# Chunked attention and a top-1 mixture of experts on one core: an early proposal for the first expert, and the turn from attention to experts in a hand-written order

## The chip, the core and the metric

One core of a Trainium2 chip runs the whole program. The metric is the device time in microseconds of one execution; lower is better. Work is spread over TensorE (PE, its weight loads shown apart as PEld), VectorE (DVE), ScalarE (ACT), GpSimd (POOL) and SyncE (SP, which here only issues DMAs).

## The reference, cut to what matters

```python
# attention: B=4, H=8, S=768, D=64, chunks of 32 queries
for c in range(nc):
    k_ctx = k[:, :, l_start:r_end]            # 16 keys to the left, 8 to the right
    k_full = np.concatenate([mem_k, k_ctx], axis=2)   # and 8 memory keys
    scores = scale * np.matmul(q_c, k_full.transpose(0, 1, 3, 2))
    a = softmax(scores)
    out[:, :, c_start:c_end] = np.matmul(a, v_full)
# mixture of experts: N=3072 tokens, D=512, E=8 experts, F=1024
logits = x @ w_gate + modality_bias[modality_id]
e_idx = np.argmax(logits, axis=1)
for e in range(E):
    mask = e_idx == e
    h = np.maximum(x[mask] @ w1[e], 0.0)
    out[mask] = gate_w[mask, None] * (h @ w2[e])
```

Only the expert of the highest logit is computed for a token, so tokens have to be grouped by expert on the chip. Counted on the reference's own inputs, three experts get tokens: expert 7 has 735 of the first two batches, 1100 of the first three and 1505 in all; expert 5 has 578, 933 and 1288; expert 2 has 223, 271 and 279.

## The kernel before, in words

**Attention.** A unit is two heads of one batch (16 units, 4 for each batch), and each unit has two half steps; the main loop (`for i in range(n + 2)`) runs over the 32 half steps and two more. In half step i TensorE does the scores of i, transposes the exponents of i-1 (`exps_t`), transposes keys (even half steps, `trans_k`) or queries (odd, `trans_q`) of the next unit, transposes the result of i-2 (`trans_x`) and multiplies the exponents of i-1 with the values (`attend`). ScalarE copies the keys out of PSUM into the block-diagonal tile `kbd` (`store_k`, four copies), the queries (`store_q`) and the results (`xT`), and computes the exponents. VectorE subtracts the maxima (`less_max`) and divides by the sums (`normalize`). GpSimd copies the overlapping rows of the values (`share_v`) and writes the results to DRAM (`xd`). The transposes share four PSUM banks (`bank`); a new one waits until the oldest user has been read.

**Routing.** When a batch's four units are done, `route(b)` is appended to a list, and `pump` takes steps from it between the pieces of attention: a VectorE step counts one, and steps that begin with TensorE work ("pe", "late") wait for the call at the end of a half step. `route` computes logits (L541, L551, L553), the one-hot of the maximum, the rank of each token within its expert (L581 to L586), then one-hot matrices `l1` and `a1` for six tiles of 128 tokens (L654, L656 on VectorE or GpSimd, L646 to L650 on ScalarE), whose product (L664) fills a table of token numbers (L665). The third batch (b = 2) also names the expert with most tokens so far; its number goes to `regs0`, from which SyncE takes the address of the first expert's weights and GpSimd the column of the table.

**Turn.** After half step 29 the rest of the third batch's routing is forced (`pump(99, True)`), `load_w(0, 0)` loads w1 of the first expert (eight pieces `raw`), and `gather(0)` fetches 256 tokens (`xg`). `conv` splits a weight piece into a high part (ScalarE, L726) and a low part (L728, VectorE, or GpSimd in four pieces). `trans` transposes the tokens, `mm1(f)` is one of eight pieces of the first layer (12 matmuls, then ReLU by ScalarE at L804 and the low part by VectorE at L807), `mm2(f)` one of the second layer (6 matmuls, L813). The routing of the fourth batch runs between these, and its table is what `gather(1)` of the next slot reads. `plan_early` and `plan_rest` choose the experts of later slots on VectorE.

**Order.** TensorE, SyncE and GpSimd run in program order everywhere. ScalarE and VectorE run in program order up to half step 26 (`MAN`) and again from `slot(1)`; between the two the framework's scheduler orders them. From slot 1 on everything is slots of `mm1` and `mm2`; a slot's weights stay in place when the next slot has the same expert (a condition on the load).

Of the kernel before, what the change touches and what calls it, by code (L numbers as in the profile page):

```python
# [40 lines left out]
NP3 = 0  # L41
NACT = 2
CPOOL = (10, 12, 13, 14, 15)
MAN = 26
KB = 3
# [8 lines left out]
def tile_chunk_attention_top1_moe(  # L54
# [51 lines left out]
    man = ExitStack()  # L106
    man.enter_context(tc.manual_schedule(engines={mybir.EngineType.Activation, mybir.EngineType.DVE}))
# [81 lines left out]
    regs0 = const.tile([1, 2], I32, name="regs0")  # L189
# [222 lines left out]
    routing, now = [], [0]  # L412

    def pump(k, pe=False):
        k *= KB if routing and routing[0][2] == B - 2 else 1
        while k > 0 and routing:
            g, wait, b, since = routing[0]
            if wait:
                if not pe or now[0] < since + (wait == "late" or b < B - 2) + (wait == "late" and b < B - 2):
                    return  # L420
                pe = False
            r = next(g, None)
            if r is None:
                routing.pop(0)
                return
            routing[0] = (g, r if r != "v" else "", b, now[0])
            k -= r == "v"
# [108 lines left out]
    def route(b):  # L536
# [51 lines left out]
        sx = sm.tile([P, NT, 1], F32, name="sx")  # L588
        nc.vector.reduce_sum(sx, ex, axis=AX.X)
        yield "v"  # L590
        nc.vector.tensor_scalar(sx, sx, 1e-9, None, op0=ALU.add)
        yield "v"
        gt = sm.tile([P, NT, XW - DM], F32, name="gt")
        nc.vector.reciprocal(gt, sx.to_broadcast([P, NT, XW - DM]))
        yield "v"
        with nc.allow_non_contiguous_dma(reason="one gate per token"):
            nc.gpsimd.dma_start(xd[b * S:(b + 1) * S, DM:XW].rearrange("(t p) c -> p t c", p=P), gt)
# [19 lines left out]
        if b == B - 2:  # L617

            cm = sm.tile([P, 1], F32, name="cm")
            cb = sm.tile([P, E], F32, name="cb")  # L620
            nc.vector.tensor_copy(cb, rk[:, NT, :])
            yield "v"
            nc.vector.reduce_max(cm, cb, axis=AX.X)
# [6 lines left out]
            yield "v"  # L630
            nc.vector.tensor_scalar(regs0[:, 0:1], cm[0:1], -1.0, float(E), op0=ALU.mult, op1=ALU.add)
            yield "v"
            nc.vector.tensor_scalar(regs0[:, 1:2], cm[0:1], -float(HI), float(E * HI), op0=ALU.mult, op1=ALU.add)
            yield "v"
# [5 lines left out]
        for t in range(NT):  # L640
# [3 lines left out]
            if b == B - 1 and NP3 <= t < NP3 + NACT:  # L644
# [6 lines left out]
                hot.append((l1, a1))  # L651
                continue
            eng = nc.gpsimd if t < (NPOOL, NPOOL, NPOOL, NP3)[b] else nc.vector
# [4 lines left out]
            hot.append((l1, a1))  # L658
        if b == B - 1:
            plan_early()  # L660
# [37 lines left out]
    def load_w(row, half):  # L698
        if half == 0:
            if row == 0:  # L700
                ev[0] = nc.values_load(regs0[0:1, 0:1], engines=[mybir.EngineType.SP], min_val=0, max_val=E - 1,
                                       skip_runtime_bounds_check_because="the place of one of 8 experts")
            else:
# [6 lines left out]
        kw = {} if row == 0 or row == ROW_X and half == 0 else {"cond": ev[row, "c"]}  # L710
# [84 lines left out]
    def mm1(f, rest=False, whole=True):  # L795
# [11 lines left out]
        nc.vector.scalar_tensor_tensor(hl[:, f], ph, 0.0, hh[:, f].bitcast(F32), op0=ALU.max, op1=ALU.subtract)  # L807
# [90 lines left out]
    for i in range(n + 2):  # L898
        live = i < n
        u, hf = units[i] if live else (NU, i % 2)  # L900
        now[0] = i
        if i == MAN:
            man.close()
# [40 lines left out]
        if i > n:  # L944
            mm1(1)
        if i > n:
            trans_x(*units[i - 2])
        if 1 <= i < n:
            normalize(*units[i - 1])
            pump(1)  # L950
        if i >= 2:
            u2, hf2 = units[i - 2]
            if hf2 == 1 and u2 % 4 == 3:
                routing.append((route(u2 // 4), True, u2 // 4, 0))
        if i == 1:
            routing.append((more_constants(), False, -1, 0))
# [5 lines left out]
        if live and hf == 0:  # L962
            if 0 < u < NU - 3:
                load_qk(u + 3)
            if u >= 1 and u - 1 + NVW < NU:
                load_v(u - 1 + NVW)
        if (u, hf) == (NU - 2, 1):
            while routing:
                pump(99, True)
# [7 lines left out]
            load_w(0, 0)  # L977
            gather(0)
        elif u == NU - 1:
            conv(2 * hf)  # L980
# [117 lines left out]
    ctx.enter_context(tc.manual_schedule(engines={mybir.EngineType.Activation, mybir.EngineType.DVE}))  # L1098
# [53 lines left out]
```

## Time and profile before

| | us |
|---|---|
| median of 3 runs (lowest to highest) | 441.83 (441.26 to 442.32) |
| the profiled execution, its own time | 439.56 |
| its span, first to last instruction | 437.8 |
| busy: PE / DVE / ACT / POOL | 413.5 / 308.4 / 269.1 / 205.5 |

The span is a single stretch of work: attention up to about 130 us, the turn up to about 169 us, then slots. A group of rows has a start in microseconds from the span's start, a duration, the engine, the line, and in brackets the idle time before it and what ended it.

### The profile page before, as it was taken

How to read it: one execution, taken by the hardware profiler on the slowest of the kernel's cores; microseconds unless marked ns; L12 is line 12 of the kernel's file. 1: busy time of each engine (PE TensorE's matmuls, PEld its weight loads, DVE VectorE, ACT ScalarE, POOL GpSimd, SP SyncE). 2: the span in 40 equal slices, each digit the busy share in tenths (PEclk: the TensorE clock that was granted, in tenths of full speed). 3: DMA queues.
4: the chain of work that ended last, by engine and by line, in shares of the span. 5: the costliest groups of instructions: out<-in, count | busy, mean ns of one | idle time of the engine just before them, and what ended most of it. 6: DMA issues, size and time to landing. Idle time of an engine off the chain costs nothing. (4 is left out here: it accounts for less than half of the span.)

```text
span 437.8 us, 11877 instructions
## 1 busy us (share of the span) xinstructions
PE 413.5 (94%) x4053; PEld 354.6 (81%) x4053; DVE 308.4 (70%) x752; ACT 269.1 (61%) x537; POOL 205.5 (47%) x409
## 2 busy tenths in 40 slices
PE   7889999999978989999999999999999999999993
PEld 4667787777756968989798998989898989898982
DVE  7788697796798799848366356767777685959530
ACT  6857878787738555747366456656656656657521
POOL 8998889798588932450154306314031115220101
PEclk9999999999999998999999999999999999999998
DMA  7779988888487110496196968414696304340101
GB/s 203 215 204 259 273 217 251 218 222 215 115 237 248 62 40 17 127 272 188 35 270 214 209 196 271 140 49 147 132 256 203 130 5 158 90 145 1 49 1 48
DMA packets 78308, 69.31 MB, mean 158 GB/s; under 512 B 36764, under 2 KB 64564, under 8 KB 78229
## 3 DMA queue, kind: packets, MB, share of 16 engines
q1 hardware_dynamic: 71488, 48.84, 40.7%
q0 software_dynamic: 5888, 19.41, 14.6%
q8 instruction: 37, 0.61, 0.6%
q14 instruction: 43, 0.34, 0.3%
q10 hardware_dynamic: 852, 0.11, 0.2%
HBM read 81.25 MB, written 16.58 MB: 223 GB/s over the span
## 5 line engine op out<-in xcount | busy, mean ns | idle before, releaser
L803 PEld LDWEIGHTS tr<-xt,w 128*128 128x128 f32 x1152 | 140.9, 189 | 4.6 <-issue 1.9
L803 PE MATMUL tr<-xt,w 128*128 128x256 f32 (+1 forms) x1152 | 142.6, 284 | 1.8 <-ACT xt L761 0.7
L813 PE MATMUL av<-wh,h 128*128 128x512 f32 x384 | 125.7, 399 | 0.0
L813 PEld LDWEIGHTS av<-wh,h 128*128 128x128 f32 x384 | 72.7, 189 | 16.8 <-issue 0.4
L807 DVE SCALAR_TENSOR_TENSOR h<-tr,h 128x256 fp32r<-128x256 f32 x96 | 40.6, 424 | 63.7 <-ACT h L804 45.5
L813 PE MATMUL av<-wl,h 128*128 128x512 f32 x192 | 76.0, 396 | 0.0
L728 DVE TENSOR_TENSOR wl<-raw,wh 128x512 fp32r<-128x512 f32 x91 | 63.3, 695 | 8.5 <-ACT wh L726 1.3
L804 ACT ACTIVATE h<-tr 128x256 fp32r<-128x256 f32 x96 | 36.9, 385 | 52.3 <-PE tr L803 46.0
L838 POOL DMA_INDIRECT out_dram<-o,ix x24 | 24.9, 1037 | 92.6 <-ACT o L834 90.2
L728 DVE TENSOR_TENSOR w<-raw,w 128x512 fp32r<-128x512 f32 x93 | 60.6, 691 | 5.1 <-DMA raw<-in_moe_w_dram 2.5
L301 POOL COPY vw<-vw 24x384 f32<-24x384 f32 (+1 forms) x128 | 60.1, 507 | 8.5 <-DMA vw<-in_v_dram 7.0
L726 ACT CAST wh<-raw 128x512 fp32r<-128x512 f32 x96 | 58.7, 615 | 0.1
L726 ACT CAST w<-raw 128x512 fp32r<-128x512 f32 x96 | 52.9, 622 | 0.0
L343 ACT COPY kbd<-tr 64x672 f32<-64x672 f32 x62 | 48.2, 778 | 4.4 <-PE tr L337 3.3
L813 PEld LDWEIGHTS av<-wl,h 128*128 128x128 f32 x192 | 36.4, 190 | 7.7
L834 ACT ACTIVATE o<-av,gate 128x512 f32<-128x512 f32 x24 | 16.3, 689 | 39.5 <-PE av L813 31.2
L746 POOL DMA_INDIRECT xg<-xd,gx x24 | 27.3, 1137 | 18.3 <-POOL gx L744 5.7
L371 ACT ACTIVATE PT<-tr 128x384 f32<-128x384 f32 x32 | 15.8, 494 | 25.9 <-PE tr L369 25.8
L381 PE MATMUL av<-vw,PT 128*32 128x130 f32 x768 | 28.4, 278 | 1.5 <-ACT PT L371 1.5
L351 PE MATMUL sc<-kbd,qT 128*32 128x128 f32 x768 | 27.4, 275 | 2.3 <-DVE kbd L343 1.3
L381 PEld LDWEIGHTS av<-vw,PT 128*32 128x32 f32 x768 | 19.7, 109 | 6.9 <-issue 4.0
L351 PEld LDWEIGHTS sc<-kbd,qT 128*32 128x32 f32 x768 | 20.6, 109 | 5.6 <-POOL kbd L325 3.0
(250 smaller groups left out, 515.6 us busy)
## 6 DMA issues: line engine op xcount, KB each, us to landing
raw<-in_moe_w_dram SPq DMA_DIRECT2D x192, 256.0 KB
k<-in_k_dram SPq DMA_DIRECT2D x16, 384.0 KB
q<-in_q_dram SPq DMA_DIRECT2D x16, 384.0 KB
xd<-xb POOLq DMA_DIRECT2D x16, 384.0 KB, 4.7
vw<-in_v_dram SPq DMA_DIRECT2D x32, 184.0 KB
xs<-xg SPq DMA_DIRECT2D x14, 256.0 KB
xq<-xs SPq DMA_DIRECT2D x28, 128.0 KB
vw<-in_mem_v_dram SPq DMA_DIRECT2D x32, 48.0 KB
```

The lines of the kernel that those rows point to most:

```text
L301: nc.gpsimd.tensor_copy(vw[r0:r0 + 24, c + 1:c + 1 + w, d], vw[r0 + 32:r0 + 56, c:c + w, d])
L343: copy(dst.rearrange("p c (i j) -> p c i j", j=2)[:, :, :, j], win)
L351: nc.tensor.matmul(sc[32 * j:32 * j + 32, t * P:(t + 1) * P], qT[:, 32 * c:32 * c + 32], kbd[:, c].rearrange("p h m -> p (h m)"), start=Tr ...
L381: nc.tensor.matmul(avb[32 * j:32 * j + 32, t * W:(t + 1) * W], PT[:, t * P + 32 * j:t * P + 32 * j + 32], vw[:, c, 0:W], start=True, stop= ...
L726: nc.scalar.copy(wh[i], raw[i])
L728: (eng or nc.vector).tensor_sub(wl[i][:, s], raw[i][:, s], wh[i][:, s].bitcast(F32))
L746: nc.gpsimd.indirect_dma_start(out=xg[t], out_offset=None, in_=xd[0:rows], in_offset=bass.IndirectOffsetOnAxis(ap=gx[:, t:t + 1], axis=0))
L803: nc.tensor.matmul(pw, wt[i][:, j * P:(j + 1) * P], x[:, c, 0:w], start=(n == 0), stop=(n == 11))
L804: nc.scalar.activation(hh[:, f], ph, AF.Relu)
L807: nc.vector.scalar_tensor_tensor(hl[:, f], ph, 0.0, hh[:, f].bitcast(F32), op0=ALU.max, op1=ALU.subtract)
L813: nc.tensor.matmul(pos[t], x, w[8 + f], start=(f == 0 and n == 0), stop=(f == 7 and n == 2))
L838: nc.gpsimd.indirect_dma_start(out=out, out_offset=bass.IndirectOffsetOnAxis(ap=to[:, t:t + 1], axis=0), in_=outs[t], in_offset=None, boun ...
```

## The change

The first slot's expert is proposed after the second batch (`rege`, `cme`, `ohe`), and its w1 is loaded in half step 26 instead of 29. The third batch keeps the proposal if that expert has at least 256 tokens by then; after half step 29 the load is issued again under the condition that the third batch chose another one. ScalarE and VectorE are in program order throughout. `pump` has a second point in each half step ("mid", before `attend`) at which TensorE work of the third batch's routing may run; `KB` is 2 instead of 3, and the second batch gets half as many steps again. The gate's sum moves behind the one-hot matrices, with a reciprocal of 6 elements and a copy by GpSimd in place of a reciprocal of 96. In the third batch, two of six one-hot tiles go to ScalarE, one (not two) to GpSimd. In the turn, `trans(0)` and `trans(1)` stand before the last `attend`; the order of `conv`, `mm1`, routing and `mm2` is written out: w2 pieces 14 and 15 are split by GpSimd (before 10, 12, 13, 14, 15), piece 7 of w1 too; the table of the fourth batch is filled after `mm2(0)` instead of after `mm2(2)`; the low parts of `mm1(5)` to `mm1(7)` come later (`lows`).

```diff
-CPOOL = (10, 12, 13, 14, 15)
-MAN = 26
-KB = 3
+KB = 2
...
-    man = ExitStack()
-    man.enter_context(tc.manual_schedule(engines={mybir.EngineType.Activation, mybir.EngineType.DVE}))
+    ctx.enter_context(tc.manual_schedule(engines={mybir.EngineType.Activation, mybir.EngineType.DVE}))
...
     def pump(k, pe=False):
-        k *= KB if routing and routing[0][2] == B - 2 else 1
+        k = k * KB if routing and routing[0][2] == B - 2 else k * 3 // 2 if routing and routing[0][2] == B - 3 else k
         while k > 0 and routing:
-            g, wait, b, since = routing[0]
+            g, wait, b, since, point = routing[0]
             if wait:
-                if not pe or now[0] < since + (wait == "late" or b < B - 2) + (wait == "late" and b < B - 2):
+                if b == B - 2 and wait is not True and now[0] < 2 * NU and now <= [since, point]:
+                    return
+                if not pe or pe == "mid" and b != B - 2 or now[0] < since + (wait == "late" or b < B - 2) + (wait == "late" and b < B - 3) or (b, wait) == (B - 2, "late") and now[0] < 2 * NU - 3:
                     return
...
-            if b == B - 1 and NP3 <= t < NP3 + NACT:
+            if b == B - 1 and t < NACT or b == B - 2 and t >= NT - NACT:
...
-            eng = nc.gpsimd if t < (NPOOL, NPOOL, NPOOL, NP3)[b] else nc.vector
+            eng = nc.gpsimd if t < (NPOOL, NPOOL, 1, 0)[b] else nc.vector
...
+        nc.vector.reciprocal(sx, sx)
+        yield "v"
+        gt = sm.tile([P, NT, XW - DM], F32, name="gt")
+        nc.gpsimd.tensor_copy(gt, sx.to_broadcast([P, NT, XW - DM]))
...
+        if i == n:
+            trans(0)
+            trans(1)
+        if i < n:
+            pump(1, "mid")
+            now[1] = 1
         if 1 <= i <= n:
             attend(*units[i - 1])
         if i == n:
             trans_x(*units[i - 2])
-            trans(0)
-            trans(1)
-            conv(4)
-            conv(5, nc.gpsimd)
             normalize(*units[i - 1])
             mm1(0)
-        if i > n:
-            mm1(1)
+            conv(4)
         if i > n:
             trans_x(*units[i - 2])
+            conv(5, nc.gpsimd)
+            mm1(1)
+            conv(6)
+            conv(7, nc.gpsimd)
...
+                if u + NVW == NU:
+                    load_w(0, 0)
...
-            while routing:
-                pump(99, True)
...
-            load_w(0, 0)
+            load_w(0, 0, checked=True)
...
     load_w(0, 1)
-    conv(6)
-    conv(7)
     pump(99, True)
+    conv(8)
+    conv(9)
     mm1(2)
     pump(99, True)
-    for f in range(3, 6):
-        mm1(f)
-    for f in range(8, 16):
-        conv(f, nc.gpsimd if f in CPOOL else None)
+    mm1(3)
+    conv(10)
+    mm1(4)
     pump(99, True)
-    mm1(6)
-    mm1(7)
+    lows = [mm1(f, low=False) for f in range(5, 8)]
     pos = [ps.tile([P, 512], F32, name="av", tag="av", bufs=2) for _ in range(2)]
-    for f in range(NEARLY):
+    mm2(0)
+    pump(99, True)
+    for f in range(11, 16):
+        conv(f, nc.gpsimd if f > 13 else None)
+        if lows:
+            lows.pop(0)()
+    for f in range(1, NEARLY):
         mm2(f)
-    pump(99, True)
```

## Rows read from the trace of the kernel before

**Rows 1.** Stages: window, length, busy PE, PEld, DVE, ACT, POOL, clock, DMA share, GB/s.
```profile
0.00:107.50 107.50, 99.16 (x1698) 77.08 (x1701) 84.70 (x248) 81.96 (x141) 94.92 (x209) 1.00 0.85 228
...
126.50:136.60 10.10, 7.68 (x147) 5.80 (x146) 7.69 (x18) 5.80 (x13) 6.56 (x12) 1.00 0.75 208
136.60:152.10 15.50, 15.48 (x130) 13.43 (x131) 12.91 (x38) 10.19 (x23) 15.48 (x30) 1.00 0.51 181
152.10:162.70 10.60, 10.58 (x50) 8.34 (x48) 10.04 (x55) 6.67 (x17) 3.83 (x9) 1.00 0.09 15
162.70:169.10 6.40, 4.14 (x15) 3.48 (x16) 6.05 (x30) 2.28 (x4) 1.54 (x5) 0.73 0.23 71
169.10:438.00 268.90, 260.02 (x1753) 233.82 (x1751) 171.09 (x307) 150.10 (x319) 69.61 (x124) 0.99 0.47 136
```

**Rows 2.** Timeline of TensorE: start, duration, line, operands, count, idle before.
```profile
102.42 0.91 PE L664 MATMUL tr<-a,l 128*128 128x192 f32 x6
...
111.80 0.55 PE L551 MATMUL tr<-ident,lgs 128*128 128x128 f32 x3 [0.38 <-ACT kbd L343]
...
122.98 0.79 PE L664 MATMUL tr<-a,l 128*128 128x192 f32 x3
...
126.25 0.35 PE L664 MATMUL tr<-a,l 128*128 128x192 f32 x1 [0.57 <-DVE a L656]
126.53 0.86 PE L351 MATMUL sc<-kbd,qT 128*32 128x128 f32 x24
...
136.62 3.54 PE L803 MATMUL tr<-xt,w 128*128 128x256 f32 x24 [0.70 <-ACT xt L761]
...
156.92 0.42 PE L813 MATMUL av<-wh,h 128*128 128x512 f32 x1
...
162.29 0.39 PE L813 MATMUL av<-wh,h 128*128 128x512 f32 x1
165.26 1.67 PE L785 MATMUL tr<-ident,xg 128*128 128x128 f32 x7 [1.09 <-DMA xg<-xd,gx]
...
169.08 11.56 PE L803 MATMUL tr<-xt,w 128*128 128x256 f32 x96
```

**Rows 3.** Timeline of ScalarE.
```profile
117.48 0.49 ACT L371 ACTIVATE PT<-tr 128x384 f32<-128x384 f32 x1 [1.97 <-PE tr L369]
118.00 3.15 ACT L343 COPY kbd<-tr 64x672 f32<-64x672 f32 x4
...
151.93 0.40 ACT L646 ACTIVATE dist<-iota,lo 128x128 f32<-128x128 f32 x1 [2.38 <-DVE lo L610]
...
153.22 0.39 ACT L646 ACTIVATE dist<-iota,lo 128x128 f32<-128x128 f32 x1
...
155.03 3.73 ACT L726 CAST w<-raw 128x512 fp32r<-128x512 f32 x7
```

**Rows 4.** Timeline of VectorE.
```profile
144.57 0.26 DVE L553 TENSOR_REDUCE l<-tr 128x24 f32<-128x96 f32 x1 [1.04 <-PE tr L551]
...
155.81 0.67 DVE L728 TENSOR_TENSOR w<-raw,w 128x512 fp32r<-128x512 f32 x1
...
158.25 0.34 DVE L665 TENSOR_TENSOR tab_i<-table,tr 128x192 int32<-128x192 f32 x1
...
168.09 1.27 DVE L762 TENSOR_TENSOR xt<-tr,xt 128x512 fp32r<-128x512 f32 x2
```

**Rows 5.** Timeline of GpSimd.
```profile
152.73 0.33 POOL L736 COPY gate<-xg 128x1 f32<-128x1 f32 x2
...
158.73 0.19 POOL L743 COPY ix<-tab_i 128x2 int32 x1 [5.67 <-DVE score L474]
```

**Rows 6.** Weight pieces `raw`, 110 to 175 us: ns least/median/most, first and last start.
```profile
L728 POOL TENSOR_TENSOR wl<-raw,wh x20: 443/450/857, 143.0 to 151.3; 128x128 fp32r<-128x128 f32 x20
L728 POOL TENSOR_TENSOR w<-raw,w x12: 444/682/962, 133.3 to 141.2; 128x128 fp32r<-128x128 f32 x12
```

**Rows 7.** Timeline of SyncE, which issues the loads.
```profile
154.33 3.09 SPq L713 DMA_DIRECT2D raw<-in_moe_w_dram  x8
```

More of the change, by code (lines that the diff above doesn't have):

```diff
@@ L40 @@
 NPOOL = 2
-NP3 = 0
 NACT = 2
-CPOOL = (10, 12, 13, 14, 15)
-MAN = 26
-KB = 3
+KB = 2
 NSPIN = 11
@@ L586, in route @@
         nc.tensor.matmul(rkf[:, 0:NT * E], tri_b, oh.rearrange("p t e -> p (t e)"), start=False, stop=True)
[L588 to L597, printed above, removed]
         pick = sm.tile(sh, F32, name="pick")
@@ L616, in route @@
         yield "v"
-        if b == B - 2:
-            cm = sm.tile([P, 1], F32, name="cm")
+        if b == B - 1:
+            nc.vector.tensor_copy(plan_new("counts"), rk[0:64, NT, :])
+            yield "v"
+        hot = []
+        for t in range(NT):
+            l1 = rt.tile([P, P], F32R, name="l1", bufs=NT)
+            a1 = rt.tile([P, 192], F32R, name="a1", bufs=NT)
+            T = b * NT + t
+            if b == B - 1 and t < NACT or b == B - 2 and t >= NT - NACT:
+                dist = sm.tile([P, 192], F32, name="dist", bufs=2)
+                nc.scalar.activation(dist[:, 0:P], iota[:, 0:P], AF.Abs, scale=-1.0, bias=lo[:, t])
+                nc.scalar.activation(l1, dist[:, 0:P], AF.Relu, scale=-1.0, bias=1.0)
+                dist = sm.tile([P, 192], F32, name="dist", bufs=2)
+                nc.scalar.activation(dist, iota, AF.Abs, scale=-1.0, bias=ac[:, t])
+                nc.scalar.activation(a1, dist, AF.Relu, scale=tokn[:, T:T + 1], bias=tokm[:, T:T + 1])
+                hot.append((l1, a1))
+                yield "v"
+                continue
+            eng = nc.gpsimd if t < (NPOOL, NPOOL, 1, 0)[b] else nc.vector
+            eng.tensor_scalar(l1, iota[:, 0:P], lo[:, t], None, op0=ALU.is_equal)
+            yield "v"
+            eng.tensor_scalar(a1, iota, ac[:, t], tokm[:, T:T + 1], op0=ALU.is_equal, op1=ALU.mult)
+            yield "v"
+            hot.append((l1, a1))
+        sx = sm.tile([P, NT, 1], F32, name="sx")
+        nc.vector.reduce_sum(sx, ex, axis=AX.X)
+        yield "v"
+        nc.vector.tensor_scalar(sx, sx, 1e-9, None, op0=ALU.add)
+        yield "v"
+        nc.vector.reciprocal(sx, sx)
+        yield "v"
+        gt = sm.tile([P, NT, XW - DM], F32, name="gt")
+        nc.gpsimd.tensor_copy(gt, sx.to_broadcast([P, NT, XW - DM]))
+        with nc.allow_non_contiguous_dma(reason="one gate per token"):
+            nc.gpsimd.dma_start(xd[b * S:(b + 1) * S, DM:XW].rearrange("(t p) c -> p t c", p=P), gt)
+        if b in (B - 3, B - 2):
+            cm = cme if b == B - 3 else sm.tile([P, 1], F32, name="cm")
             cb = sm.tile([P, E], F32, name="cb")
@@ L709, in load_w @@
         e = ev[row]
-        kw = {} if row == 0 or row == ROW_X and half == 0 else {"cond": ev[row, "c"]}
+        kw = {} if row == 0 and not checked or row == ROW_X and half == 0 else {"cond": ev[row, "c"]}
         for f in range(8):
@@ L793, in trans_rest, with mm1 @@
         nc.vector.tensor_sub(xtl[:, :, 256:], t, xth[:, :, 256:].bitcast(F32))
-    def mm1(f, rest=False, whole=True):
+    def mm1(f, rest=False, whole=True, low=True):
         w = 256 + (NR if rest else 0)
@@ L806, in mm1, with lower @@
             nc.scalar.activation(hq[:, f], pw[:, 256:], AF.Relu)
-        nc.vector.scalar_tensor_tensor(hl[:, f], ph, 0.0, hh[:, f].bitcast(F32), op0=ALU.max, op1=ALU.subtract)
+        def lower():
+            nc.vector.scalar_tensor_tensor(hl[:, f], ph, 0.0, hh[:, f].bitcast(F32), op0=ALU.max, op1=ALU.subtract)
+        if not low:
+            return lower
+        lower()
     def mm2(f, tiles=(0, 1)):
@@ L900, in tile_chunk_attention_top1_moe @@
         u, hf = units[i] if live else (NU, i % 2)
-        now[0] = i
-        if i == MAN:
-            man.close()
+        now[:] = i, 0
         if live and i < n - 1:
@@ L976, in tile_chunk_attention_top1_moe @@
             hh, hl = [xp.tile([P, 8, 256], F32R, name=f"h{i}") for i in range(2)]
-            load_w(0, 0)
+            load_w(0, 0, checked=True)
+            if routing and routing[0][1] == "late":
+                pump(1, True)
+            assert not routing or not routing[0][1]
             gather(0)
         elif u == NU - 1:
+            pump(99)
             conv(2 * hf)
```

56 lines of the change are left out of this document (27 added, 29 removed).

## The prediction

> **What bounds the kernel now.** I read the stages first [rows 1]. From 169.1 us on TensorE works 260 of 269 us at clock 0.99, and before 107.5 us it works 99 of 107.5. Both ends are TensorE's own work, which the change leaves as it is, so a gain or loss made between carries to the end one to one. The loose stretch lies between: TensorE has 7.7 of 10.1 us in 126.5 to 136.6 and 4.1 of 6.4 in 162.7 to 169.1, where the granted clock falls to 0.73. The timeline of TensorE then shows three places [rows 2]. First, the table product L664 of the third batch: six matmuls that take 0.91 us together in an earlier batch run from 122.98 to 126.53, each waiting for a one-hot tile from VectorE. Second, the expert's first matmul at 136.62. Third, the wait for the tokens of slot 1: TensorE is done at 162.6 (162.29 plus 0.39), gets the last tokens at 165.26, runs eight transposes and six matmuls at the low clock and reaches steady slots at 169.08. GpSimd's rows [rows 5] tell why: it stood ready from 153.06 and waited 5.67 us for the table. Third view, VectorE: 10.04 of 10.6 us and 6.05 of 6.4 us busy [rows 1]; from 155.81 to 168.09 [rows 4] it has hardly a gap. So behind the wait for tokens a second bound stands close.
>
> I count after M, the start of the scores of half step 30, at 126.53 before [rows 2]. The slots' start is M + 42.55.
>
> **Part 1, up to M.** The mid point takes the transposes L551 of the third batch to before `attend(25)` and all later steps half a step or more forward; the one-hot tiles are done in half step 28 and L664 runs in 29 without waiting. That removes 3.55 - 0.9 = 2.65 us. But two tiles go to ScalarE, and by the step counts (two for each pump unit) they land in half step 28 between the exponents (117.48) and the four key copies (3.15 us) [rows 3]. One tile takes 153.22 - 151.93 = 1.29 us, two 2.6. ScalarE is already on end there. Its chain becomes exponents 0.5, tiles 2.6, copies 3.15, a result copy 0.4, exponents 0.5, then TensorE's L664 0.85 and `attend` 0.8 (estimates from the neighbours of rows 2): 117.48 + 8.8 = 126.3. The stall is not removed, it moves to the key copies, whose banks `exps_t(28)` and `trans_q` wait for. The start of that chain can shift: L551's second half waited 0.38 us for a key copy at 111.80 [rows 2]. At the mid point it comes 0.8 us sooner and waits either for the first half's reduction (all 0.4 us earlier) or still for the copy (0.4 us later, with `attend` now behind it). So M moves by -0.8 to +0.2; I take -0.4. What the mid point queues behind a wait is `attend(25)` and the next scores.
>
> **Part 2, M to the experts.** The early load puts eight issues behind the last value load on SyncE, where nothing follows until half step 29. Counts from the reference's inputs make the proposal expert 7 after two batches (735 of 1536), and it keeps it with 1100 after three, so the second load is skipped: before, eight skipped issues of slot 1 took 3.09 us [rows 7] while DMA was at 0.09 [rows 1]. It costs nothing on the path, since w2's load waits for the end of attention anyway. In return the gather of the first tokens no longer shares the DMA engines (0.75 there [rows 1]). GpSimd reaches that gather at the same time after M as before, because the gate's copy and the value copies stand in front. The transposes before the last `attend` hide the casts that TensorE waited 0.70 us for [rows 2]. So the first expert matmul comes at M + 9.4 instead of M + 10.1.
>
> **Part 3, the fourth batch.** A piece of `mm1` takes 12 x 11.56 / 96 = 1.45 us, a matmul of `mm2` 5.37 / 23 = 0.233 [rows 2]. TensorE transposes the logits at about M + 15.5, but VectorE, now in program order, first has the low parts of pieces 8 and 9 and of `mm1(2)`, behind ScalarE's casts (3.73 / 7 = 0.53 each [rows 3]): it starts at M + 17.5 (bounds 16.2, right after the transposes, and 18.0, as at 144.57 before [rows 4]). From there to the first one-hot tile on ScalarE it was 151.93 - 144.57 = 7.36 us [rows 3, 4]. The change takes the gate's sum and reciprocal, three low parts and the planner's first steps out of it and puts one subtraction of 0.67 in; 4.5 us is my estimate, and 7.4 stays as the far end. So ScalarE has its two tiles from M + 22.0 to 24.6, three ReLUs to 25.6 and pieces 11 to 14 at M + 27.7. TensorE: rank at M + 19.8, `mm1(5)` to `mm1(7)`, `mm2(0)` and L664 end at M + 26.6; VectorE fills the table at M + 27.0, against 158.25 (M + 31.7) before [rows 4]. That is 4.7 us gained.
>
> **Part 4, where that gain goes.** GpSimd no longer waits for the table: in its program order pieces 14 and 15, eight subtractions, stand between the gate and the next gather, and piece 14 is ready at M + 27.7. At 0.45 us each (the group of 20, [rows 6]) they end at M + 31.3, and half a microsecond of small copies (an estimate, two of them are 0.33 [rows 5]) puts the gather at M + 31.9; before, it was 158.73 = M + 32.2. At the other end, 0.68 each (the group of 12, [rows 6]), it is M + 33.8. I take M + 32.5, nearer the first, since only three subtractions of VectorE fall beside them. From the gather to the slots' start it was 169.08 - 158.73 = 10.35 us [rows 2, 5], and TensorE is done with its `mm2` at about M + 35.0, before the tokens, so this wait stays: M + 42.85, 0.3 us late. VectorE gives the second figure. From 144.57 to 155.81 it took 11.24 us [rows 4] with some 0.5 of waiting; it now gets four subtractions more (10 to 13, 2.7 us) and the table (0.34), and loses a low part and most of a reciprocal (about 1.0): 12.8, so slot 1's own work starts at M + 30.3 instead of 29.3, and the low part of the next tokens, at 168.09 = M + 41.6 before, comes 0.7 us later. It was not late then by some 0.9 us, so it decides only if it slips further.
>
> The 0.45 against 0.68 is a row before it is a rule: the 12 pieces ran beside VectorE's subtractions, the 20 mostly not [rows 6]. The Trainium skill, SBUF — State Buffer, section "Who interferes with whom", says a VectorE instruction with two SBUF inputs locks out a GpSimd instruction that reads SBUF, and the other way round, for a whole instruction; by that rule pieces 14 and 15 would run nearer 0.68 beside pieces 12 and 13, and it speaks against this order.
>
> **Part 5, the rest.** The first two batches get a few more VectorE steps for each half step, a copy on GpSimd for a reciprocal on VectorE, and seven small steps for the proposal. VectorE has 84.7 of 107.5 us there, GpSimd 94.9 [rows 1], TensorE is the bound: nothing, with -0.3 to +0.3 as bounds, a microsecond or more if GpSimd falls behind with the value copies.
>
> **The sum.** -0.4 (part 1) + 0.3 (part 4; parts 2 and 3 are used up in its wait) = -0.1 us. On the span that is 437.7 of 437.8; the profiled execution took 439.56, which is 2.3 below the median of 441.83, so the same difference on the median gives 441.7.
>
> **The rivals.** *The turn works.* If the eight subtractions run at 0.45, VectorE's chain is as short as estimated or shorter and M takes its early end, the gather is issued near M + 30 and the tokens come within a microsecond of M + 35. Then the clock does not fall, which saves half of the transposes' 1.67 us and, of the 2.15 us that follow them up to 169.08, all but the 6 x 0.233 = 1.4 of six matmuls: 1.6 us [rows 2]. With M's early end that is 1.5 to 3 us in all: 439.5. For it: the table is early by 4.7 us. Against it: VectorE's 12 us of slot 1's work.
>
> *GpSimd's two pieces decide, slower.* Place: pieces 14 and 15 ahead of `gather(1)`. Price: 8 x 0.23 = 1.9 us at the contended duration, and up to 2.9 more if VectorE's chain takes 7.4 instead of 4.5. It decides as soon as the last subtraction ends later than M + 31.6. Less what part 1 gives: 443.6. For it: [rows 6], and VectorE's 10.04 of 10.6 [rows 1]. Against it: two pieces on GpSimd are fewer than the five before.
>
> *The proposal is not kept.* Then w1 is loaded twice, the second time as late as before: no gain, no loss, 441.8. The counts leave it 2 in 100; it is in "same".
>
> **How the numbers follow.** Two runs of this kernel differ by up to about 0.2%, 0.9 us; less counts as the same. My forecast, no difference (441.0 to 442.7): 0.43. The turn works: 0.32. GpSimd or ScalarE decide the other way: 0.25. The range holds most of both rivals: 439.0 to 443.8, the upper end by 1.9 of the second price, the lower by the clock.
>
> **What would show it.** Right: L664 of the third batch without a gap, but a wait of 2 us or more of `exps_t` or `trans_q` on `store_k` before M; the table some 4 to 5 us earlier after M, and GpSimd's gather behind its last subtraction (no wait for VectorE there); TensorE still waiting 3 us or more for the tokens, the clock still falling. Wrong: no ScalarE wait in half steps 28 and 29 (then M is 2 us earlier), the gather directly behind the table, the clock at 1.00 through the opening slot, or a difference before 107 us.

## The result and the profile after

The changed kernel takes 444.66 us (median of 7 runs, 443.72 to 446.12), the kernel before beside it 441.26 (7 runs, 439.75 to 442.32): a ratio of 1.0077, with a 95% interval of 1.0053 to 1.0102. It is slower by some 3.4 us, where I forecast no difference. The profiled run took 444.68 us with a span of 442.9.

First the stages of after, cut at the same events as [rows 1] (columns as there: window, length, busy time of TensorE, its weight loads, VectorE, ScalarE, GpSimd, then the granted clock, the DMA share and GB/s).

```profile
0.00:109.20 109.20, 99.73 (x1697) 77.21 (x1701) 84.81 (x253) 82.04 (x141) 94.44 (x211) 1.00 0.85 227
109.20:127.85 18.65, 15.34 (x272) 12.64 (x268) 13.86 (x56) 15.04 (x31) 12.39 (x25) 1.00 0.70 187
127.85:137.60 9.75, 7.56 (x155) 5.76 (x147) 8.52 (x24) 5.50 (x11) 8.10 (x14) 1.00 0.51 141
137.60:152.50 14.90, 14.68 (x132) 13.23 (x130) 11.98 (x41) 9.29 (x24) 5.60 (x9) 1.00 0.51 169
152.50:163.10 10.60, 10.59 (x50) 8.38 (x48) 9.98 (x42) 7.93 (x17) 7.18 (x15) 1.00 0.04 6
163.10:172.90 9.80, 4.46 (x15) 3.69 (x16) 9.31 (x46) 2.28 (x4) 3.84 (x7) 0.74 0.21 55
172.90:442.90 270.00, 261.24 (x1753) 234.92 (x1751) 170.79 (x306) 149.80 (x319) 68.80 (x124) 0.99 0.46 135
```

The last row but one is the place where most is lost: the wait for slot 1's tokens, 6.4 us long before, is 9.8 us long now, at a clock of 0.74 (0.73 before), and VectorE is busy in 9.31 of it. The timeline of TensorE shows what lies at its ends (start, duration, line, operands, count, and the idle time before it with what ended it).

```profile
122.33 0.55 PE L368 MATMUL tr<-ident,sb 128*128 128x128 f32 x3 [1.01 <-DVE cb L648]
124.58 0.55 PE L314 MATMUL tr<-ident,qr 128*128 128x128 f32 x3 [1.70 <-ACT kbd L342]
...
126.34 0.89 PE L681 MATMUL tr<-a,l 128*128 128x192 f32 x6
...
127.85 0.84 PE L350 MATMUL sc<-kbd,qT 128*32 128x128 f32 x24
...
137.59 1.66 PE L823 MATMUL tr<-xt,w 128*128 128x256 f32 x12
...
162.69 0.40 PE L838 MATMUL av<-wh,h 128*128 128x512 f32 x1
167.22 0.33 PE L805 MATMUL tr<-ident,xg 128*128 128x128 f32 x1 [4.13 <-DMA xg<-xd,gx]
168.77 1.75 PE L805 MATMUL tr<-ident,xg 128*128 128x128 f32 x7 [1.23 <-DMA xg<-xd,gx]
...
172.89 12.38 PE L823 MATMUL tr<-xt,w 128*128 128x256 f32 x96
```

These answer to [rows 2]: M is 127.85, the table product L681 (L664 before) now runs in one piece, the first expert matmul stands at M + 9.74, the slots start at 172.89 = M + 45.04 instead of M + 42.55, and the first 96 matmuls of the slots take 12.38 us instead of 11.56, because the clock stays low beyond the transposes (0.50 from 168 to 172 us, 0.55 from 172 to 175). GpSimd's timeline, against [rows 5] and [rows 6], and VectorE's, against [rows 4]:

```profile
156.40 5.34 POOL L748 TENSOR_TENSOR wl<-raw,wh 128x128 fp32r<-128x128 f32 x8 [1.93 <-ACT wh L746]
...
162.07 0.18 POOL L763 COPY ix<-tab_i 128x2 int32 x1
```

```profile
154.96 0.34 DVE L682 TENSOR_TENSOR tab_i<-table,tr 128x192 int32<-128x192 f32 x1
...
158.02 0.67 DVE L748 TENSOR_TENSOR w<-raw,w 128x512 fp32r<-128x512 f32 x1
...
171.46 1.27 DVE L782 TENSOR_TENSOR xt<-tr,xt 128x512 fp32r<-128x512 f32 x2
```

The table is ready at M + 27.1, 4.6 us sooner than before. GpSimd doesn't look at it until M + 34.2, since pieces 14 and 15 stand ahead: no wait for VectorE is left in its row, it is late by its own work. The next tokens' low part L782 starts at M + 43.6, 2 us later than before.

**Where the 3.4 us come from.** The start of a half step is the start of its scores (S17, S26; S30 is M). The slots start with the first matmul of slot 2 (L823, L803 before). The differences between these, from the same rows of each trace, tell more than the times themselves: S17 alone lies at 73.3 and 75.9 us in two traces of the same kernel before, with the clock at 1.00 and 0.76 from 20 to 30 us.

| kernel (trace) | S17 to S26 | S26 to M | M to slots | slots to end |
|---|---|---|---|---|
| before | 34.21 | 19.04 | 42.55 | 268.7 |
| before, second trace | 34.20 | 19.02 | 42.41 | 268.9 |
| after | 35.48 | 18.65 | 45.04 | 270.0 |
| after, second trace | 35.96 | 20.19 | 44.36 | 269.4 |
| gather first | 35.81 | 19.54 | 45.34 | 270.6 |
| no tiles on ScalarE | 36.37 | 19.60 | 44.42 | 269.0 |
| early pace of before | 34.54 | 20.20 | 44.20 | 270.0 |
| planner's last steps later | 35.68 | 19.59 | 44.25 | 268.9 |
| gather first, steps later | 35.84 | 19.93 | 37.76 | 272.1 |
| the same, pieces 6 and 7 on GpSimd | 36.10 | 19.84 | 37.13 | 274.0 |
| planned turn | 35.46 | 20.18 | 45.16 | 270.1 |
| keys first | 35.87 | 19.35 | 44.56 | 269.7 |
| all cures | 35.88 | 17.88 | 37.84 | 270.0 |
| before with the cured turn | 34.34 | 19.02 | 38.49 | 269.6 |

(For the gather first, the slots' start is taken behind the wait that interrupts them, at 174.89.) So the loss has three places: 1.3 to 1.8 us between half steps 17 and 26, -0.4 to +1.2 before M, and 1.9 to 2.5 in the turn with 0.5 to 1.3 behind it, most of that in slot 2 at the lower clock (0.8 in the first trace, 12.38 against 11.56). In the two traces they add up to 4.7 and 5.4, more than the 3.4 of the medians. The first 17 half steps, which differ by up to 2.8 us among all traces (S17 from 73.28 to 76.06), can hide that much; what they are in the runs without a trace isn't known.

### The profile page after: what moved, and what is told of

Read it like the earlier page. It is cut to its first block, busy times and chain, and to the rows that moved or that the text cites. A ratio compares the mean times of both kernels' runs of the same rounds, so it can differ in the third digit from the quotient of the medians.

```text
span 442.9 us, 11921 instructions
## 1 busy us (share of the span) xinstructions
PE 413.6 (93%) x4053; PEld 355.8 (80%) x4053; DVE 309.3 (70%) x762; ACT 271.9 (61%) x545; POOL 200.4 (45%) x403
## 5 line engine op out<-in xcount | busy, mean ns | idle before, releaser
L823 PEld LDWEIGHTS tr<-xt,w 128*128 128x128 f32 x1152 | 142.1, 189 | 3.8 <-issue 2.2
L823 PE MATMUL tr<-xt,w 128*128 128x256 f32 (+1 forms) x1152 | 143.7, 285 | 1.2 <-PEq L1153 0.6
L748 DVE TENSOR_TENSOR wl<-raw,wh 128x512 fp32r<-128x512 f32 x94 | 65.3, 696 | 8.4 <-ACT wh L746 1.1
L766 POOL DMA_INDIRECT xg<-xd,gx x24 | 26.4, 1100 | 19.5 <-PE tr L805 6.8
L370 ACT ACTIVATE PT<-tr 128x384 f32<-128x384 f32 x32 | 15.8, 494 | 24.4 <-PE tr L368 24.2
```

What stands on the lines that cost most here:

```text
L748: (eng or nc.vector).tensor_sub(wl[i][:, s], raw[i][:, s], wh[i][:, s].bitcast(F32))
L766: nc.gpsimd.indirect_dma_start(out=xg[t], out_offset=None, in_=xd[0:rows], in_offset=bass.IndirectOffsetOnAxis(ap=gx[:, t:t + 1], axis=0))
L823: nc.tensor.matmul(pw, wt[i][:, j * P:(j + 1) * P], x[:, c, 0:w], start=(n == 0), stop=(n == 11))
```

## The experiments

Every ratio is to the kernel before, run beside; the changed kernel's is 1.0077 (1.0053 to 1.0102).

**The kernel before, a second time.** No edit; for the scatter.

> The kernel before, unchanged, for a second trace. It shows how much of the 1.7 us by which the changed kernel is late at half step 26 (its scores start at 109.20 against 107.49) is only the spread between executions. If the early loss is the change's own, half step 26 starts at 107.3 to 107.9 here and half step 30 at 126.4 to 127.0. If it is spread, half step 26 starts somewhere in 107.5 to 109.2.

442.15 us. The first two rows of the table differ by 0.14 us or less in the first three columns, but everything is 2.6 us later from S17 on: half step 26 starts at 110.10, beyond both expectations. So of the traces only differences within each are read below.

**Is it GpSimd's order? The gather first.**

```diff
     for f in range(11, 16):
-        conv(f, nc.gpsimd if f > 13 else None)
+        if f > 13:
+            nc.scalar.copy(wh[f], raw[f])
+        else:
+            conv(f)
...
         begin(row, opening, rest_next)
+        if opening:
+            for f in (14, 15):
+                for c in range(0, 512, P):
+                    cs = slice(c, c + P)
+                    nc.gpsimd.tensor_sub(wl[f][:, cs], raw[f][:, cs], wh[f][:, cs].bitcast(F32))
```

> The changed kernel with one edit: GpSimd's eight subtractions of w2's pieces 14 and 15 stand behind the gather of slot 1 instead of ahead of it. Theory (these two pieces hold the gather): the gather's first copy follows the table within 0.5 us, at about 155.5 instead of 162.1, the tokens land at about 162, the pieces end at about 163 and hold mm2(7) by 1 to 2 us; VectorE's steps of slot 1 then become the bound, since its subtractions of the next tokens come at about 170.5, so the slots start at 170 to 171 instead of 172.9, the clock stays nearer 1, and the time is 2 to 3.5 us below the changed kernel. Rival (VectorE alone sets the end of the turn): the gather comes early too, but the slots start at 172 or later and the time is within 0.8 us of the changed kernel.

446.92 us (446.3 to 448.04), ratio 1.0117 (1.004 to 1.0193). The gather's first copy came 0.4 us behind the table and TensorE got the tokens without a wait. But then (TensorE, GpSimd, VectorE):

```profile
166.51 1.10 PE L823 MATMUL tr<-xt,w 128*128 128x256 f32 x8
174.89 7.36 PE L823 MATMUL tr<-xt,w 128*128 128x256 f32 x40 [7.28 <-DVE xt L782]
```

```profile
160.24 3.36 POOL L1087 TENSOR_TENSOR wl<-raw,wh 128x128 fp32r<-128x128 f32 x8
```

```profile
159.76 3.46 DVE L440 TENSOR_SCALAR tail<-tail 64x8 f32<-64x8 f32 x1
...
174.16 1.27 DVE L782 TENSOR_TENSOR xt<-tr,xt 128x512 fp32r<-128x512 f32 x2
```

The eight matmuls on the high part of the tokens run at M + 37, the ninth waits 7.28 us for VectorE's low part. One small step L440, 0.28 us elsewhere, took 3.46 beside GpSimd's eight subtractions; without it L782 would come at about 171, still over 3 us late. The slots' start is the rival's (172 or later), the time neither's: 2.3 us above the changed kernel, though the two intervals overlap. GpSimd's order was a bound, and VectorE's program order is a second one right behind it.

**Are ScalarE's two tiles of the third batch at fault?**

```diff
-            if b == B - 1 and t < NACT or b == B - 2 and t >= NT - NACT:
+            if b == B - 1 and t < NACT:
...
-            eng = nc.gpsimd if t < (NPOOL, NPOOL, 1, 0)[b] else nc.vector
+            eng = nc.gpsimd if t < (NPOOL, NPOOL, NPOOL, 0)[b] else nc.vector
```

> The changed kernel with one edit: in the third batch no one-hot tile goes to ScalarE, and two instead of one to GpSimd, as before the change. Theory (the two tiles on ScalarE delay the key copies, for whose banks TensorE waits): the key copies of half step 28 start at about 119.0 instead of 122.2, TensorE's waits of 1.01 and 1.70 us in half step 29 go, half step 30 starts 2 to 2.7 us earlier relative to half step 26 (18.65 us after it in the changed kernel, 16 to 16.7 here), and the time is 1.5 to 2.7 us lower. Rival (VectorE's and GpSimd's tiles come late instead): TensorE waits at the table product of half step 29 and half step 30 starts within 0.7 us of the changed kernel's.

445.76 us (444.27 to 446.51), ratio 1.0079 (1.0049 to 1.0109). The waits of 1.01 and 1.70 us are down to a quarter of a microsecond each, and 2.05 us of waiting for VectorE's `xb` stand at the token transposes instead:

```profile
127.80 0.88 PE L403 MATMUL tr<-ident,xb 128*128 128x128 f32 x3 [2.05 <-DVE xb L395]
```

S26 to M is 19.60, with the lower clock behind that wait, and the time is no lower.

**Is it the pace of the first two batches?**

```diff
-        k = k * KB if routing and routing[0][2] == B - 2 else k * 3 // 2 if routing and routing[0][2] == B - 3 else k
+        k = k * KB if routing and routing[0][2] == B - 2 else k
...
-            pump(1, "mid")
+            if routing and routing[0][2] == B - 2:
+                pump(1, "mid")
```

> The changed kernel with the pace of the first two batches' routing put back: the mid point takes steps only for the third batch, and the second batch has no half as many steps again. Theory (more VectorE steps in each half step push the subtraction and the result of attention back, for which TensorE waits): half step 26 starts 0.7 to 1.5 us earlier than in the changed kernel (109.20), and the time is 0.7 to 1.5 us lower. Rival (the early loss is spread between executions, or the gate's copy on GpSimd): half step 26 starts within 0.4 us of the changed kernel's, and the time is the same.

443.92 us (441.64 to 445.31), ratio 1.0038 (1.0002 to 1.0074). Half step 26 starts at 109.10, within the rival's 0.4 us of the changed kernel's, but only because S17 came 0.8 us later in this trace: S17 to S26 falls to 34.54, 0.3 above before. So most of the 1.3 to 1.8 us is the pace. Whether the time falls is less clear, since the intervals of the two ratios overlap. In after part of it comes as waits of a quarter of a microsecond, of which before has one in half step 23 (TensorE's timeline of after):

```profile
96.86 0.55 PE L368 MATMUL tr<-ident,sb 128*128 128x128 f32 x3 [0.24 <-DVE sx L634]
97.65 1.05 PE L314 MATMUL tr<-ident,qr 128*128 128x128 f32 x6 [0.24 <-ACT kbd L342]
98.94 0.55 PE L403 MATMUL tr<-ident,xb 128*128 128x128 f32 x3 [0.25 <-DVE xb L395]
```

**Is VectorE alone the bound of the turn?** Four planner steps stay ahead of the low part, the last three come behind it.

```diff
                 conv(f)
-                next(steps, None)
+                if f < 4:
+                    next(steps)
...
             conv(6)
-            next(steps, None)
             trans(0)
```

> The changed kernel, with the planner's last steps on VectorE (2.4 us by the trace of after: L502 to L522) moved from ahead of the next tokens' low part L782 to behind it; GpSimd's order is left. Theory G (the tokens are late because pieces 14 and 15 stand ahead of the gather on GpSimd, and VectorE only keeps pace): L782 may start up to 2 us earlier after its transposes, but TensorE still waits 4 to 5.5 us for the tokens, the slots start at M + 44.5 to 45.0 and the time stays at 444 to 445. Theory V (VectorE's program order alone sets the slots' start): the slots start 2 us earlier, M + 43, and the time is 442.5.

445.29 us (443.56 to 447.8), ratio 1.0073 (1.0039 to 1.0108). VectorE's L782 starts at M + 42.1, 1.5 us sooner than in after, but TensorE still waits 3.89 and 1.26 us for tokens, as theory G has it, and the slots start at M + 44.25:

```profile
167.51 0.33 PE L805 MATMUL tr<-ident,xg 128*128 128x128 f32 x1 [3.89 <-DMA xg<-xd,gx]
```

One bound taken away alone gains nothing, from this side either.

**Both together.** The gather first with pieces 14 and 15 on VectorE, and all planner steps but the first in slot 2 behind its first matmuls, with slot 2's gather behind them; the next expert's pieces 6 and 7 come behind the token transposes.

```diff
-        conv(f, nc.gpsimd if f > 13 else None)
+        conv(f)
...
+        if row == 2:
+            for f in range(8):
+                mm1(f)
+                if f < 4:
+                    next(steps, None)
+                    next(steps, None)
+                if f == 3:
...
+                    begin(row, opening, rest_next)
...
             if opening:
+                if f == 0:
+                    next(steps)
                 conv(f)
-                next(steps, None)
```

> The changed kernel with both cured: the gather first on GpSimd with pieces 14 and 15 on VectorE, and all but the first of the planner's steps moved from ahead of the next tokens' low part to the first matmuls of slot 2 (where the gather of slot 2 moves behind them). Theory of two bounds (GpSimd's order first, VectorE's program order right behind it): neither the 4.13 us wait for tokens nor the 7.28 us wait for the low part of the kernel with the gather first comes back; the slots start at M + 37 to 38.5 with the clock up, slot 2 loses 0 to 2 us because its gather is later, and the time is 437 to 440. Rival (a third bound, ScalarE's copies or the transfer of the tokens): the slots start later than M + 41 and the time stays above 442.

443.16 us (441.25 to 446.22), ratio 1.0013 (0.9979 to 1.0047): faster than the changed kernel and not different from before; the traced run took 441.45. The slots start at M + 37.76, 7 us sooner than in after, at a clock of 1.00 throughout the turn. TensorE's rows show where 2.8 us of it go back:

```profile
167.46 10.10 PE L823 MATMUL tr<-xt,w 128*128 128x256 f32 x84
177.74 1.69 PE L823 MATMUL tr<-xt,w 128*128 128x256 f32 x12 [0.18 <-DVE h L829]
...
185.21 0.30 PE L805 MATMUL tr<-ident,xg 128*128 128x128 f32 x1 [1.18 <-DMA xg<-xd,gx]
186.68 0.55 PE L805 MATMUL tr<-ident,xg 128*128 128x128 f32 x3 [1.17 <-DMA xg<-xd,gx]
```

Slot 2's gather, now behind the planner's last step at 179, is waited for, and slot 2 takes 27.0 us instead of 24.2. The expected 437 to 440 was missed; of the causes the trace shows this one and S26 to M, 19.93 with the lower clock; why other runs lie up to 4.8 us above the traced one it doesn't show.

**With help from GpSimd.** As the last, but `conv(6, nc.gpsimd)` and `conv(7, nc.gpsimd)`.

> As the kernel with the gather first and the steps later, but the next expert's pieces 6 and 7 are subtracted on GpSimd behind the gather instead of on VectorE. Theory of contention: these eight subtractions take 0.6 us or more each beside VectorE's, VectorE's own become longer, and nothing is gained against that kernel (-0.3 to +2 us). Rival (GpSimd is free help there): VectorE ends 1.2 us sooner, slot 2's gather too, and the time is 0.5 to 1.5 us lower than that kernel's.

443.62 us (440.77 to 446.25), ratio 1.0004 (0.9961 to 1.0047): no difference from the last that can be measured. GpSimd's eight subtractions took 6.73 us, 0.84 each, as the theory of contention has it (0.6 or more).

**The change without its turn.** From w2's load to slot 1 the order of before: ScalarE and VectorE planned, pieces 10 and 12 to 15 on GpSimd.

> The change without its turn: the early proposal, the two points for each half step and ScalarE's tiles of the third batch stay, but from w2's load to slot 1 the order is that of the kernel before (planned, pieces 10 and 12 to 15 on GpSimd, no low parts held back). Theory (the loss lies in the turn): M minus the start of half step 26 is 18.65 +- 0.3, the slots start at M + 42 to 43, and the time is 440.5 to 442. Rival (the loss lies ahead of M or in the transposes ahead of the last attend): the slots start at M + 44 or later, or half step 26 starts over 1.5 us late, and the time is 443 to 445.

444.39 us (442.78 to 448.8), ratio 1.0012 (0.9978 to 1.0046). The ratio fits the theory, but the time and the trace don't: the slots start at M + 45.16, as the rival has it. The gate, which the change moved behind the one-hot tiles, came behind all of GpSimd's 20 subtractions there, but the gather, at M + 34.4, still waited 3.96 us for the table, and that came at M + 33.9 (M + 31.7 before, [rows 4]). The planned order with the moved gate isn't the planned order of before, and the profiled run (448.8) was the longest of ten. This run decides nothing.

**The stall ahead of M.** In half step 28 the planner steps come behind the key copies; one tile on ScalarE, two on GpSimd; `cb` is copied as soon as the ranks are read.

```diff
-            pump(3)
+            if i != 28:
+                pump(3)
             store_k(u + 1, 1, 0, nc.scalar.copy)
...
+        if i == 28:
+            pump(7)
...
-            if b == B - 1 and t < NACT or b == B - 2 and t >= NT - NACT:
+            if b == B - 1 and t < NACT or b == B - 2 and t == NT - 1:
...
-            eng = nc.gpsimd if t < (NPOOL, NPOOL, 1, 0)[b] else nc.vector
+            eng = nc.gpsimd if t < (NPOOL, NPOOL, NPOOL, 0)[b] else nc.vector
```

> The changed kernel with only its attention end altered, the turn is left: in half step 28 the planner steps come behind the four key copies and the token transposes, the third batch has one tile on ScalarE and two on GpSimd, and the copy of the ranks' last row, which held a bank until L648, is made directly behind the first reading of that bank. Theory (the stall of 1.01 + 1.70 us ahead of M is ScalarE's tiles in front of the key copies and a bank held by the late copy, and where TensorE's clock falls behind it, it costs 1 us more): those waits shrink to 1.5 us together or less, the clock stays at 1.00 from 120 to 132 us, M minus the start of half step 26 is 16.5 to 17.8 instead of 18.65 to 20.2, the way from M to the slots stays at 44.5 to 45, and the time is 441.5 to 443.5. Rival (the stall is the chain of ScalarE as a whole, and moves on to another wait): M minus S26 is 18.5 or more and the time stays at 444 to 445.

445.79 us (445.22 to 449.41), ratio 1.0138 (1.0091 to 1.0185). M minus S26 is 19.35, as the rival has it: of both waits a quarter of a microsecond is left, and one of 2.36 us stands half a step's work later, at the token transposes. The row names ScalarE's copies of the queries, the first of which ended at 126.20; VectorE's `xb`, which the transposes read, ended at 126.17. So this trace doesn't tell which of the two held them:

```profile
126.31 0.87 PE L403 MATMUL tr<-ident,xb 128*128 128x128 f32 x3 [2.36 <-ACT qT L319]
```

```profile
125.70 0.89 ACT L319 COPY qT<-tr 128x384 f32<-128x384 f32 x2
```

```profile
125.61 0.56 DVE L395 TENSOR_TENSOR xb<-av,den 128x384 f32<-128x384 f32 x1
```

With the run without ScalarE's tiles that makes three forms of one stall: 2.71 us at the bank and the key copies, 2.05 and 2.36 us at the token transposes. In half step 28 the third batch's tiles, gate and proposal come in one piece, and in each of the three ways to share them out TensorE waits.

**All cures.** Both together, attention end and turn, and slot 2's transposes two pieces of `mm2` later (`if f - late in (2, 3)` with `late` 2 in slot 2).

> The kernel with the gather first and the planner's steps later, with the altered attention end as well, and with slot 2's transposes two pieces of mm2 later, so that its later gather is not waited for. Theory of three places (the key copies ahead of M, GpSimd's and VectorE's order in the turn, slot 2's gather): M minus S26 is 16.5 to 17.8, the slots start at M + 37 to 38.5, slot 2 takes 23.5 to 24 us instead of 27.0, and the time is 437 to 439.5, below both kernels. Rival (what is won early is given back later, VectorE in slot 2 being behind by then): slot 2 takes 25.5 us or more and the time is 441 or more.

439.08 us (437.34 to 440.83), ratio 0.9956 (0.9929 to 0.9983): faster than both. Slot 2 is back to 24.27 us, so the late gather was the cause there. M came at S26 + 17.88 with the wait still there:

```profile
126.01 0.52 PE L403 MATMUL tr<-ident,xb 128*128 128x128 f32 x3 [2.33 <-ACT qT L319]
```

The same code up to M had taken 19.35 in the run before, where the granted clock was 0.57 from 126 to 130 us; here it was 1.00. So the altered attention end is worth 0.8 us where the clock stays up (18.65 in after; one trace each), and in the run before the lower clock hid that. The next but one shows this difference in after itself.

**Before with the cured turn.** The kernel before up to `load_w(0, 1)`, then the cured turn and slot 2.

> The kernel before up to the turn, with the turn of the cured kernel: the order by hand of the changed kernel, but the gather first, pieces 14 and 15 on VectorE, the planner's steps behind the next tokens' low part, slot 2's transposes later. Theory (the order by hand of the turn is sound, what cost the time was which queue the gather and the low part stood in): M minus S26 is 19.0 +- 0.3, the slots start at M + 37.5 to 39 instead of 42.5, slot 2 takes 23.5 to 24 us and the time is 436.5 to 439, faster than before by 0.7 % or more. Rival (the planned order of the turn was as good as any, because something common to all, such as the logits' start, sets it): the slots start at M + 41 or later and the time is 441 or more.

437.59 us (436.4 to 439.21), ratio 0.9923 (0.9894 to 0.9952): the best of all. GpSimd, then TensorE, then the stage:

```profile
156.19 0.71 POOL L743 COPY ix<-tab_i 128x2 int32 x1 [4.36 <-DVE tab_i L665]
```

```profile
163.91 1.04 PE L785 MATMUL tr<-ident,xg 128*128 128x128 f32 x8
...
166.18 9.96 PE L803 MATMUL tr<-xt,w 128*128 128x256 f32 x84
```

```profile
163.90:166.20 2.30, 2.30 (x16) 2.02 (x15) 2.09 (x4) 1.66 (x4) 1.22 (x2) 1.00 0.00 0
```

GpSimd waits for the table again, as in [rows 5], TensorE no longer for tokens, and the clock stays up. The slots start at M + 38.49, 4.1 us sooner than before; by the ratio 3.4 us of that is in the time. Slot 2 takes 24.23 us here, against 23.43 before: 0.8 is given back. Set beside all cures, this run holds what the rest of the change is worth in the traces: 1.5 us more from S17 to S26, 1.1 less up to M, 0.7 less from there to the slots, 0.4 more behind them. These cancel, and no run tests the early proposal by itself.

**After, a second time.** No edit; was its M typical?

> The changed kernel itself, traced a second time, to see whether its first trace was typical ahead of M. Theory (the stall of some 2.9 us in one half step is long enough that TensorE's clock falls behind it in most executions, and the first trace was one of the few in which it did not): the granted clock is at or near 0.50 in 124 to 129 us, L681 takes 1.5 us instead of 0.89, M minus the start of half step 26 is 19.4 to 20.2. Rival (the other kernels' lower clock comes from their own edits): the clock stays at 1.00 there and M minus S26 is 18.4 to 18.9. By both the slots start at M + 44.5 to 45.1 and the time is 444 to 446.

445.62 us (444.09 to 446.17), ratio 1.0089 (1.0056 to 1.0122). It was not:

```profile
123.17 0.55 PE L368 MATMUL tr<-ident,sb 128*128 128x128 f32 x3 [0.97 <-DVE cb L648]
125.45 1.68 PE L314 MATMUL tr<-ident,qr 128*128 128x128 f32 x6 [1.73 <-ACT kbd L342]
126.92 0.85 PE L403 MATMUL tr<-ident,xb 128*128 128x128 f32 x3
127.42 1.58 PE L681 MATMUL tr<-a,l 128*128 128x192 f32 x6
```

The waits are the same, 0.97 and 1.73, but the six matmuls behind them take 1.58 us instead of 0.89. The stage 124 to 130 us, of the second trace and of the first:

```profile
124.00:130.00 6.00, 4.55 (x35) 4.02 (x39) 2.98 (x13) 4.23 (x8) 5.37 (x12) 0.58 0.88 241
```

```profile
124.00:130.00 6.00, 5.06 (x79) 3.80 (x82) 4.12 (x19) 3.95 (x9) 4.90 (x12) 1.00 0.89 236
```

35 instructions against 79. Of the eight traces with this attention end unaltered (after twice, and the six variants of other things), seven show the lower clock in this place; M then comes at S26 + 19.5 to 20.2, against 18.65 in the one without. Of the three with the end altered (one wait of 2.05 to 2.36 us) two show it. Of three traces with the attention end of before, whose table product waits three times for some 0.6 us (the last of them in [rows 2]), none does.

## Why the prediction was wrong

**The sum** (-0.1 us against +3.4) had its sign right in part 4, and in part 1 in one trace of after alone; it was too small in each term that it took near the favourable end, and it put the first two batches and the clock behind the turn at nothing.

**Part 1, up to M: the mechanism held, the price didn't.** "The stall is not removed, it moves to the key copies": L681 runs without a gap, and `trans_q` waits 1.70 us for a key copy. The first trace gives -0.39 where I took -0.4, which looked like proof and was luck. Two things were left out. A second wait of 1.01 us, by its row for a bank that `cb` (L648) holds until behind the tiles; I priced the proposal's seven steps but not what their place keeps occupied. And the clock: a stall in two pieces of 1.0 and 1.7 us was followed by the lower level in seven traces of eight, which costs 1.5 us between the two traces of after (18.65 and 20.19). My range ended at +0.2.

**Part 2, M to the experts: right.** M + 9.4 forecast, 9.74 and 9.12 measured, 10.09 before. It is used up in the wait, as said.

**Part 3, the fourth batch: right.** The table at M + 27.0 forecast, 27.1 measured.

**Part 4 is the step that failed.** The order was read rightly (pieces 14 and 15 ahead of the gather), but the eight subtractions were priced too low: I put the gather at M + 32.5, nearer to 0.45 us for each than to 0.68, "since only three subtractions of VectorE fall beside them". They took 5.34 / 8 = 0.67. Beside them stood not three but four weight subtractions, two low parts and ten planner steps: I had these steps in VectorE's sum and not among what GpSimd shares its time with. They also began at M + 28.55, 0.85 later than worked out. The gather came at M + 34.2 instead of 32.5, just beyond my far end of 33.8. The Trainium skill, SBUF — State Buffer, section "Who interferes with whom", had spoken for that far end (two inputs in SBUF on VectorE against GpSimd's reads); by that rule the trace agrees, 0.67. From the gather to the slots it was 10.8 us, not 10.35, so the slots start at M + 45.04 where I had M + 42.85; these 2.2 us are the largest single miss of the first trace. The clock then stayed low in slot 2's matmuls, which cost another 0.8 us that I had not counted: here the longer wait cost more than its length.

**VectorE's second figure was right and mattered more than I gave it.** Slot 1's own work starts at M + 30.2 (30.3 forecast). "It decides only if it slips further": it slipped to M + 43.6, 1.3 beyond the forecast, and the run with the gather first shows that it then stands 7.28 us in the way of a TensorE that is ready (some 3.2 of them by L440's long row in that run).

**Part 5 was wrong.** "Nothing, with -0.3 to +0.3 as bounds"; it is 1.3 to 1.8 us, most of it the pace of the second batch, as the run with the pace of before shows; the prediction's own sign of being wrong, "a difference before 107 us", was there. VectorE's and GpSimd's shares of the whole stretch (84.7 and 94.9 of 107.5) could not tell this: the quarter-microsecond waits shown above stand where one result is due, however free the engine is on average.

**The rivals.** "GpSimd's two pieces decide, slower" was what happened in the turn: it was priced at 1.9 us and up to 2.9 more, and the turn lost 1.9 to 2.5. I gave it 0.25 where its own rows [rows 6] spoke for it. Its 443.6 lay below the result because part 1 stood in it as a gain and part 5 not at all (and its own terms, 441.8 + 1.9 - 0.4, give 443.3). "The turn works" came true only with both queues changed, and then for more than its 1.5 to 3 us. With the upper ends that I had written for these two (+0.2 and +0.3) it would have been 444.5; the range ended at 443.8 because I added the bounds of one unknown alone.

What stays open: where the 0.3 us lies that S17 to S26 keeps with the pace of before, why the table came so late in the order by plan with the moved gate, what the order by hand on ScalarE and VectorE from half step 26 to M costs or gains (no run puts it back alone), and when the clock falls behind a stall and when not.

## What to carry to other kernels

When a result is wanted sooner, follow it into the program order of the engine that takes it up: work ahead of it there has to move too, priced at the duration that it has beside the other engine's work. If two queues end within a microsecond of each other, a change to either alone can show nothing, as in two runs here, and a test of one alone will seem to refute it; change both before the idea is given up. And many short waits that are turned into one long one are not the same cost: look at the granted clock behind it, in more than one trace.

## What the runs showed of the hardware

VectorE and GpSimd held each other up for far longer than one instruction. With the gather first, VectorE's L440, on 64 x 8 elements, took 3.46 us beside eight subtractions of GpSimd that ran back to back (its row and theirs stand there). It began 0.5 us ahead of the first of them, while GpSimd still issued the gather, and ended only as the last began. The other way round, with the steps later, GpSimd's two copies of a gate, 0.30 us elsewhere, took 3.94 us, 3.82 of them the first copy, which ended only behind VectorE's six subtractions:

```profile
162.87 3.94 POOL L756 COPY gate<-xg 128x1 f32<-128x1 f32 x2
```

```profile
162.95 3.69 DVE L748 TENSOR_TENSOR w<-raw,w 128x512 fp32r<-128x512 f32 x6
```

The Trainium skill, SBUF — State Buffer, section "Who interferes with whom", says that the one that comes later is blocked for a whole instruction of the other. The second pair of rows agrees in kind. In both the blocked engine waited not for one instruction of the other (0.42 and 0.62 us here) but for nearly the whole row.
